# A cosformer attention and MLP-mixer kernel: one load of v moved down its queue, one sum moved behind another, two features moved to ScalarE

## The chip, the cores and the metric

The kernel runs on one core of a Trainium2 chip. The metric is the device time of the kernel in microseconds (us): 267.13 us before the change, the median of 7 runs (266.34 to 269.36). The engines are called PE (TensorE, matrix products), DVE (VectorE), ACT (ScalarE), POOL (GpSimd) and SP (SyncE, which here only issues DMA transfers).

## What is computed

Eight batches (0 to 7 here and in the code, so the seventh is batch 6) of 576 rows and 8 heads of width 64 go through a linear attention, and its output goes through an MLP mixer:

```python
def phi(x, c, s):
    r = np.maximum(x, 0.0)
    return np.concatenate([r * c, r * s], axis=-1)
q_p = phi(q, cos_w, sin_w)
k_p = phi(k, cos_w, sin_w)
kv = np.einsum('bhsf,bhsd->bhfd', k_p, v)
z = np.sum(k_p, axis=2)
num = np.einsum('bhsf,bhfd->bhsd', q_p, kv)
den = np.einsum('bhsf,bhf->bhs', q_p, z)[..., None] + 1e-06
...
h = np.maximum(xt @ w_tok1, 0.0) @ w_tok2
u = x + h.transpose(0, 2, 1)
h2 = np.maximum(u @ w_ch1, 0.0) @ w_ch2
return (u + h2).astype(np.float32)
```

Here x is num/den with the heads side by side (512 channels), and xt is x with rows and channels exchanged. The widths are 256 for the token part (w_tok1, w_tok2) and 1536 for the channel part (w_ch1, w_ch2).

## The kernel before

**Data and tiles.** Each batch has 576 rows: four blocks of 128 rows and a tail of 64. The tails of two batches share a block, so tails are collected in `u_tail` and go through the channel part together at the very end. Inputs are loaded in f32 (k and q into two buffers each, v into one only, `vt`), turned into bf16 features (`kp`, `qp`: relu and a scale by the cosine or sine table, `feat`, lines 445 and 447) and casts (`vbf`, `cast`, line 264).

**Stages of one batch.** `kvm` multiplies features of k with v on PE; `turnx` transposes the q features by DMA into `qpT` (issued by SP, line 469); `numf`/`numfo` give num and den on PE (line 505) and x on DVE (lines 524 to 528); `mix` and `um` are the token part on PE (lines 548 and 575), with B as its hidden layer; `uo` (line 580, DVE) adds x and gives `u`; `ubc` casts `u` to bf16 `ub`, one half on POOL and one on ACT; `utx` transposes each half by DMA into `uT` (line 587, SP). `tm`, `to` and, for odd batches, `tb` do the same for the tail, `tb` with another DMA transpose (line 618). Then comes the channel part of the batch: twelve hidden blocks `c_ps` (line 711), each of four matmuls from `uT` and `wc1`, with a relu by ACT or DVE, and the second layer.

**The second layer as seven products.** The class `Seven` splits the second layer into 2x2 blocks and uses seven products of half size instead of eight (`p1` to `p7`, line 330), with sums on DVE and POOL around them. Each of the products has 12 matmuls of 256 columns. Their order is p1, p4, p2, p5, p6, p7, p3. What matters here: `sums` forms `s1` and `s2` (lines 321, 322), `s3` forms a21 (line 325); p4 ends with the sum into `u21` (line 366, DVE); p2 ends with the sum into `u11` (line 344, DVE); p5 reads `s1`, then ACT copies its result to `vc` (line 370), DVE writes a new `s1` (line 371, the block sum that p3 reads) and POOL adds `vc` to `u22` (line 372). p6 and p7 end with the DVE sums of lines 376, 377, 381 and 384 and a POOL sum (line 383), p3 with line 350. The results p1, p4, p5, p6 and p7 each ask for a bank of PSUM from a pool of four that the hidden blocks use as well.

**What sets the order.** Each engine, and SP's queue of DMA issues, works through its instructions in program order. The program order is written by hand. Up to batch 1's channel part it is the word list `PLAN`: each word is one piece of one batch, and its last letter is the engine (A for ACT, D for DVE, P for POOL). From there on six periods p = 2 to 7 and a tail follow. A period runs `channel` for batch p. It has 20 slots, one after each of the twelve hidden blocks, one after each product and one at the end; `hooks_for` hangs work of other batches on the slots: n = p+1 (numerators, mix, u, `utx` at slots 10 and 12), m = p+2 (casts at slots 3 to 7, features, `turnx` at slots 12, 14 and 15) and the loads of nxt = p+3 (k and q at slot 0, v at slot 16 or 9). The stores of batch p are issued by SP from p7 and p3, slots 17 and 18. The first block `c_ps` of a period needs the whole `uT` of its batch, made in the period before.

The lines around the load of v and around the fourth and fifth product:

```python
at(16 if nxt == 5 else 9, load, nxt, "v")
...
self.product(self.bank("E"), self.a22, t4, True)
nc.vector.tensor_add(self.u21, self.ps["E"], self.u21)
...
self.product(self.bank("C"), self.s1, t1, True)
nc.scalar.copy(self.vc, self.ps["C"])
nc.vector.tensor_sub(self.s1, self.a12, self.s2)
nc.gpsimd.tensor_add(self.u22, self.u22, self.vc)
```

Of the kernel before, what the change touches and what calls it, by code (L numbers as in the profile page):

```python
# [45 lines left out]
up.1.4 upo.1.9.A numf.2.1 up.1.2 numfo.2.1 upo.1.4.A o.0.1 up.1.5 numf.2.0 upo.1.5.A upo.1.2.A numfo.2.0 tq.1.D  # L46
feat.3.q.3.2.0.A feat.3.q.1.2.0.A feat.3.q.2.2.0.A ld.3.v.2.v22 cast.3.4.1.2.P up.1.10 up.1.3 numf.2.2
mix.2.0.2 numfo.2.2 tq.2.D upo.1.10.A up.1.8 up.1.6 numf.2.4 feat.3.q.2.2.1.A upo.1.8.A mix.2.1.2 mix.2.2.2 up.1.1
numfo.2.4 feat.3.q.1.2.1.A mix.2.3.2 mix.2.4.2 mixo.2.2.A feat.3.q.3.2.1.A upo.1.3.D tq.4.D m.1.sums.2.5 turnx.3.2.2
feat.3.q.4.2.1.D upo.1.1.D up.1.7 feat.3.q.0.2.0.A upo.1.6.A up.1.11 upo.1.7.A upo.1.11.A feat.3.k.2.2.0.D  # L50
feat.3.q.4.2.0.A feat.3.q.0.2.1.A turnx.3.4.1 um.2.1 um.2.0 m.1.p1 feat.3.k.4.2.1.A cast.3.1.1.2.P uo.2.1 ubc.2.1 uo.2.0
ubc.2.0 utx.2.1 m.1.sums.0.2 feat.3.k.0.2.1.A m.1.sums.5.6 m.1.s3 turnx.3.0.2 utx.2.0 ld.4.q.2 tb.1
cast.3.0.1.2.A m.1.p4 feat.3.k.0.2.0.A feat.3.k.4.2.0.A cast.3.3.1.2.P m.1.p2 cast.3.2.1.2.P feat.3.k.1.2.0.A
ld.4.v.2.k22 m.1.p5 ld.4.k.2.k32 feat.3.k.2.2.1.A m.1.p6 feat.3.k.3.2.1.A feat.3.k.3.2.0.A feat.3.k.1.2.1.A
m.1.p7 m.1.p3 tm.2 to.2
"""

# [1 line left out]
def kernel(  # L59
# [11 lines left out]
    nc = tc.nc  # L71
# [194 lines left out]
    def relu(eng, dst, src):  # L266
        if eng == "A":
            nc.scalar.activation(dst, src, AF.Relu)  # L268
        else:
            nc.vector.tensor_relu(dst, src)  # L270
# [32 lines left out]
    class Seven:  # L303
# [53 lines left out]
        def p4(self):  # L357
            if self.fine:
                E = [psA.tile([P, D2], F32, name="m2_ps", tag="psA") for _ in range(2)]
                for jj in range(2):  # L360
                    self.product(E, self.a22, t4, True, (jj,))
                    nc.vector.tensor_add(self.u21[:, jj], E[jj], self.u21[:, jj])
                self.store(2, self.u, 2, slice(0, D2))
            else:
                self.product(self.bank("E"), self.a22, t4, True)
                nc.vector.tensor_add(self.u21, self.ps["E"], self.u21)

        def p5(self):
            self.product(self.bank("C"), self.s1, t1, True)
# [327 lines left out]
    def channel(uT, u, store, by_slot, hooks, fine=False):  # L697
        h1 = one.tile([P, NCH, 4 * P], BF16, name="h1")
        m = Seven(h1, u, store, fine)
        slot = 0  # L700

        def step():
            nonlocal slot
            for f in hooks.get(slot, ()):
                f()
            slot += 1

        for mi in range(NCH):
            c_ps = psM.tile([P, 512], F32, name="c_ps", tag="psM")
            for ki in range(NCC):  # L710
                nc.tensor.matmul(c_ps, wc1[:, ki, mi * P:(mi + 1) * P], uT[:, :, ki, :],  # L711
                                 start=(ki == 0), stop=(ki == NCC - 1))
            relu(by_slot[mi], h1[:, mi, :], c_ps)
            if mi == NCH - 2:
                m.sums(0, K2 - 2)
            if mi == NCH - 1:
                m.sums(K2 - 2, K2)
            step()
        order = (m.p1, m.p5, m.p6, m.p7, m.p3, m.p2, m.p4) if fine else (m.p1, m.p4, m.p2, m.p5, m.p6, m.p7, m.p3)
        for f in order:  # L720
            f()
            if f == m.p1:
                m.s3()
            step()
        step()

    bt = [Batch(b) for b in range(B)]
# [10 lines left out]
    def hooks_for(n, m, nxt):  # L738
        h = {}

        def at(slot, f, *a):
            h.setdefault(slot, []).append(lambda: f(*a))
        if nxt is not None:
            at(0, load, nxt, "k")
            at(0, load, nxt, "q")
            at(16 if nxt == 5 else 9, load, nxt, "v")
        if n is not None:
            at(0, n.kv_all)
            for j in range(JA):
                at(2 + j, n.num_all, j)  # L750
            for j in range(JA):
                at(7 + j // 3, n.mix, j, 2)
            at(8, n.mix_out)
            at(10, n.u_all, 0)
            at(10, n.u_all, 1)
            at(12, n.ubc, 1, "A")
            at(12, n.utx, 1)
            at(18, n.u_all, 2)
        if m is not None:
            for j in range(JA):  # L760
                at(3 + j, m.cast, j, 1, 2, "P")
            for i, slot in enumerate((1, 2, 3, 4, 7, 7, 9, 10, 11, 12)):
                at(slot, m.feat, "q", i // 2, 2, i % 2, "A")
            for i, slot in enumerate((7, 7, 8, 8, 13, 14, 15, 16, 17, 17)):
                at(slot, m.feat, "k", i // 2, 2, i % 2, "D" if i < 4 else "A")
            at(12, m.turnx, 0, 2)
            at(14, m.turnx, 2, 2)
            at(15, m.turnx, 4, 1)
        return h
# [3 lines left out]
    for p in range(2, B):  # L773
        s = bt[p]
        n = bt[p + 1] if p + 1 < B else None
        m = bt[p + 2] if p + 2 < B else None
        nxt = p + 3 if p + 3 < B else None
        channel(s.uT, s.u, store_batch(p), evac if n else evac2, hooks_for(n, m, nxt))
    channel(uT_tail, u_tail, store_tail, evac2, {}, fine=True)

    _ = tile, bass_utils
# [30 lines left out]
```

## Time and profile before

| what | us |
|---|---|
| median of 7 runs (lowest, highest) | 267.13 (266.34, 269.36) |
| the profiled execution | 266.49 |
| its span, first to last instruction | 264.7 |
| mean granted clock of PE, as a share | 0.999 |
| period p=2, first block to the next period's | 88.01 to 114.40 |
| period p=3 | 114.40 to 142.02 |
| period p=4 | 142.02 to 168.42 |
| period p=5 | 168.42 to 194.98 |

The profile is of one execution. A row of groups gives an engine, a line of the kernel, an operation with its tiles, how often it ran and for how long. A wait is put down to what came last. The chain of waits goes back from the last instruction, at each step to what released it; the share of PE in it is 84%, of DVE 6% and of DMA 6%. SP is only an issuer: its rows show when a transfer was issued, not when it landed; the time from issue to landing is given apart. Matmuls are pipelined, so the distance between two starts says more than one's length: 0.216 for 512 columns, 0.109 for 256.

### The profile page before, as it was taken

To read this page: it belongs to the slowest core of one execution; us is meant where nothing else is said; L and a number is where in the kernel's file an instruction comes from. 1 tells how busy PE (TensorE), PEld (TensorE's weight loads), DVE (VectorE), ACT (ScalarE), POOL (GpSimd) and SP (SyncE) were. 2 spreads that over 40 slices of the span, in tenths; PEclk is the share of its full clock that TensorE was granted. 3 is DMA by queue.
4 is the path that set the end of the run, shared out by engine and by line. 5 is a ranking of instruction groups with operands and counts; after the bars stand their busy time and mean duration, and the time that the engine had idled before them with its cause. 6 is when DMAs were issued, how large, how long until landed. Compare 5 with 4: busy or idle time off the path is not lost.

```text
span 264.7 us, 5569 instructions
## 1 busy us (share of the span) xinstructions
PE 252.6 (95%) x2201; PEld 164.2 (62%) x2217; DVE 205.4 (78%) x377; ACT 150.7 (57%) x244; POOL 62.1 (23%) x78
## 2 busy tenths in 40 slices
PE   6887999999999999999998999999999999999993
PEld 2776556456558655865585548754875486486482
DVE  6389797799999787879885868886878488476484
ACT  2787263473779396948683778586854342323320
POOL 2083070040036112321436002440230023003020
PEclk9999999999999999999999999999999999999999
DMA  6999999999979999999999997950594042202104
GB/s 199 360 249 172 256 263 234 365 217 256 370 209 172 250 350 387 229 191 324 291 318 202 283 368 176 162 195 2 106 173 160 2 79 96 85 0 85 76 1 160
DMA packets 79434, 53.41 MB, mean 202 GB/s; under 512 B 47792, under 2 KB 77232, under 8 KB 79408
## 3 DMA queue, kind: packets, MB, share of 16 engines
q1 hardware_dynamic: 74688, 48.77, 69.2%
q0 software_dynamic: 4144, 3.77, 9.4%
q10 hardware_dynamic: 576, 0.52, 0.6%
q8 instruction: 17, 0.28, 0.4%
q14 instruction: 9, 0.07, 0.1%
HBM read 35.85 MB, written 9.44 MB: 171 GB/s over the span
## 4 chain that ended last, share of the span: by engine, by line
PE 84%; DVE 6%; DMA 6%; issue 2%; DVEq 0%
PE c_ps L711 28%; PE m_ps L330 22%; PE c L627 8%; PE b L548 6%; PE u L575 5%; PE kv L476 4%; PE o L639 4%; DMA kt<-in_k_dram 3%; PE nf L505 3%; DMA uT<-ub 3%; DVE kp L447 1%; PE tr L460 1%; PE ut L603 1%; PE nm L505 1%; DVE x L528 1%
## 5 line engine op out<-in xcount | busy, mean ns | idle before, releaser
L711 PE MATMUL c_ps<-uT,wc 128*128 128x512 bf16 x288 | 70.4, 379 | 1.1 <-DMA uT<-ub 1.1
L268 ACT ACTIVATE h<-c_ps 128x512 bf16<-128x512 f32 x66 | 38.8, 595 | 50.8 <-PE c_ps L711 36.2
L711 PEld LDWEIGHTS <-wc 128*128 128x128 bf16 x336 | 30.6, 97 | 34.0 <-issue 2.0
L330 PEld LDWEIGHTS <-h 128*128 128x128 bf16 x384 | 37.5, 98 | 6.1
L445 ACT ACTIVATE qp<-qt,cos_t 128x512 bf16<-128x512 f32 x35 | 24.7, 720 | 15.0 <-DMA qt<-in_q_dram 11.8
L330 PEld LDWEIGHTS <-s 128*128 128x128 bf16 x288 | 28.0, 98 | 4.1 <-DVE s L371 0.7
L264 POOL CAST vbf<-vt 128x512 bf16<-128x512 f32 (+3 forms) x29 | 19.2, 699 | 45.1 <-DMA vt<-in_v_dram 45.1
L270 DVE TENSOR_SCALAR h<-c_ps 128x512 bf16<-128x512 f32 x18 | 12.4, 688 | 19.7 <-PE c_ps L711 19.7
L264 POOL CAST ub<-u 128x1024 bf16<-128x1024 f32 x9 | 9.7, 1075 | 68.5 <-DVE u L580 68.4
L330 PE MATMUL m_ps<-wc,s 128*128 128x256 bf16 x192 | 23.6, 273 | 0.4 <-DVE s L371 0.4
L330 PE MATMUL m_ps<-wc,h 128*128 128x256 bf16 x192 | 23.6, 273 | 0.0
L330 PE MATMUL m_ps<-t,h 128*128 128x256 bf16 x192 | 23.6, 273 | 0.0
L445 ACT ACTIVATE qp<-qt,sin_t 128x512 bf16<-128x512 f32 x32 | 22.9, 721 | 0.0
L627 PE MATMUL c<-uT,wc 128*128 128x512 bf16 x96 | 22.7, 379 | 0.1
L528 DVE TENSOR_TENSOR x<-nf,den 128x512 bf16<-128x512 f32 x30 | 20.7, 691 | 1.0
L505 PEld LDWEIGHTS <-qpT 128*128 128x128 bf16 x320 | 15.3, 98 | 9.6 <-DVE x L528 1.5
L548 PE MATMUL b<-x,w 128*128 128x512 bf16 (+1 forms) x84 | 19.8, 354 | 0.3
L580 DVE TENSOR_TENSOR u<-u,x 128x1024 f32<-128x1024 f32 x16 | 18.9, 1217 | 0.9 <-PE u L575 0.8
L372 POOL TENSOR_TENSOR u<-u,vc 128x512 f32<-128x512 f32 x7 | 9.5, 1356 | 35.4 <-ACT vc L370 35.4
L445 ACT ACTIVATE kp<-kt,sin_t 128x512 bf16<-128x512 f32 x23 | 16.0, 713 | 1.7 <-DVE u L580 1.5
L447 DVE TENSOR_SCALAR kp<-kt,cos_t 128x512 bf16<-128x512 f32 x18 | 10.6, 596 | 8.1 <-DMA kt<-in_k_dram 8.1
L445 ACT ACTIVATE kp<-kt,cos_t 128x512 bf16<-128x512 f32 x22 | 15.3, 712 | 0.8 <-DMA kt<-in_k_dram 0.8
(117 smaller groups left out, 389.9 us busy)
## 6 DMA issues: line engine op xcount, KB each, us to landing
out_dram<-u SPq DMA_DIRECT2D x32, 256.0 KB, 3.3
qt<-in_q_dram SPq DMA_DIRECT2D x8, 640.0 KB, 7.6
kt<-in_k_dram SPq DMA_DIRECT2D x8, 640.0 KB, 8.2
qt<-in_q_dram SPq DMA_DIRECT2D x8, 512.0 KB, 6.5
kt<-in_k_dram SPq DMA_DIRECT2D x8, 512.0 KB, 7.1
vt<-in_v_dram SPq DMA_DIRECT2D x6, 640.0 KB, 8.8
vt<-in_v_dram SPq DMA_DIRECT2D x6, 512.0 KB, 7.4
wc<-in_moe_w_ch_dram POOLq DMA_DIRECT2D x4, 384.0 KB, 8.1
```

The costliest lines, as they stand in the source:

```text
L264: (nc.scalar.copy if eng == "A" else ENG[eng].tensor_copy)(dst, src)
L268: nc.scalar.activation(dst, src, AF.Relu)
L330: nc.tensor.matmul(ps[jj] if isinstance(ps, list) else ps[:, jj], a[:, ki, jj * P:(jj + 1) * P], b[:, ki], start=(first and ki == 0 and (j ...
L445: nc.scalar.activation(dst, src, AF.Relu, scale=tab)
L447: ENG[eng].tensor_scalar(dst, src, scalar1=tab, scalar2=0.0, op0=ALU.mult, op1=ALU.max)
L505: nc.tensor.matmul(nm[:, hh * (D + 1):(hh + 1) * (D + 1)], self.qpT[:, j * H + h, :], self.kv[:, h, :D + 1], start=(not eps or hh == 0), s ...
L528: nc.vector.tensor_mul(dst, nmv[:, :, :, :D], den_b)
L548: nc.tensor.matmul(b1[:, mi], w1[:, col(self.c, j), mi * P:(mi + 1) * P], self.x[:, j, cs], start=(j == 0 and (g == 2 or mi == 0)), stop=( ...
L575: nc.tensor.matmul(ps[:, jj], w2[:, ki, 1 + 2 * g + jj, :], self.B1[:, ki, :], start=(ki == 0), stop=(ki == NT - 1))
L580: nc.vector.tensor_add(self.sb("u")[:, js, :], self.ps.pop(("u", g)), self.x[:, js, :])
L627: nc.tensor.matmul(ps, wc1[:, ki, mi * P:(mi + 1) * P], self.uT[:, :, ki, :], start=(ki == 0), stop=(ki == NCC - 1))
L711: nc.tensor.matmul(c_ps, wc1[:, ki, mi * P:(mi + 1) * P], uT[:, :, ki, :], start=(ki == 0), stop=(ki == NCC - 1))
```

## The change

Three edits. The load of v for batch 6 (nxt = 6, issued in period p=3) goes from slot 9 to slot 16; batch 5's stays at 16 and batch 7's at 9. The sum into `u21`, which ended p4, becomes a function of its own, `u21_out`, and is called after p5, without a slot of its own, in every period and in the plan; the tail (`fine`) keeps its own. In the plan two features of batch 3 go from DVE to ACT and stand earlier: `feat.3.q.4.2.1` and `feat.3.k.2.2.0`, now ahead of the last two pieces of batch 2's mix.

```diff
-numfo.2.4 feat.3.q.1.2.1.A mix.2.3.2 mix.2.4.2 mixo.2.2.A feat.3.q.3.2.1.A upo.1.3.D tq.4.D m.1.sums.2.5 turnx.3.2.2
-feat.3.q.4.2.1.D upo.1.1.D up.1.7 feat.3.q.0.2.0.A upo.1.6.A up.1.11 upo.1.7.A upo.1.11.A feat.3.k.2.2.0.D
+numfo.2.4 feat.3.q.1.2.1.A feat.3.k.2.2.0.A feat.3.q.4.2.1.A mix.2.3.2 mix.2.4.2 mixo.2.2.A feat.3.q.3.2.1.A upo.1.3.D tq.4.D m.1.sums.2.5 turnx.3.2.2
+upo.1.1.D up.1.7 feat.3.q.0.2.0.A upo.1.6.A up.1.11 upo.1.7.A upo.1.11.A
...
-ld.4.v.2.k22 m.1.p5 ld.4.k.2.k32 feat.3.k.2.2.1.A m.1.p6 feat.3.k.3.2.1.A feat.3.k.3.2.0.A feat.3.k.1.2.1.A
+ld.4.v.2.k22 m.1.p5 m.1.u21_out ld.4.k.2.k32 feat.3.k.2.2.1.A m.1.p6 feat.3.k.3.2.1.A feat.3.k.3.2.0.A feat.3.k.1.2.1.A
...
                 self.product(self.bank("E"), self.a22, t4, True)
-                nc.vector.tensor_add(self.u21, self.ps["E"], self.u21)
+
+        def u21_out(self):
+            nc.vector.tensor_add(self.u21, self.ps["E"], self.u21)
...
-        order = (m.p1, m.p5, m.p6, m.p7, m.p3, m.p2, m.p4) if fine else (m.p1, m.p4, m.p2, m.p5, m.p6, m.p7, m.p3)
+        order = (m.p1, m.p5, m.p6, m.p7, m.p3, m.p2, m.p4) if fine else (m.p1, m.p4, m.p2, m.p5, m.u21_out, m.p6, m.p7, m.p3)
         for f in order:
             f()
             if f == m.p1:
                 m.s3()
-            step()
+            if f != m.u21_out:
+                step()
...
-            at(16 if nxt == 5 else 9, load, nxt, "v")
+            at(9 if nxt == 7 else 16, load, nxt, "v")
```

## The prediction

> **What bounds the kernel now.** I read the page's busy table first, then PE's waits, then the chain of waits around each of them, then SP's issue timeline.
>
> ```profile
> PE 252.6 (95%) x2201; PEld 164.2 (62%) x2217; DVE 205.4 (78%) x377; ACT 150.7 (57%) x244; POOL 62.1 (23%) x78
> ```
>
> PE is busy for 252.6 of 264.7 us and holds 84% of the chain: another engine counts only where it makes PE wait. PE's waits from 60 us to the end are two:
>
> ```profile
> PE c_ps L711 <- DMA uT<-ub: 1.1, 1, 1.1
> PE m_ps L330 <- DVE s L371: 0.4, 1, 0.4
> ```
>
> Matmul ends are modelled, so I measure the loss between starts. At the first, the single `ut` matmul started at 140.58 and `c_ps` at 142.02; undisturbed (168.21 to 168.42) that step is 0.21. Loss 1.23 us. At the second, the last matmul of `p7` started at 85.41 and `p3` at 86.09, where 0.11 is normal. Loss 0.57 us. These two are all that this change can take away. The chain around the first (start, us, what):
>
> ```profile
> 131.35 3.71 PE m_ps L330 x35
> 135.07 6.82 DMA uT<-ub
> 141.89 0.14 issue
> 142.02 1.02 PE c_ps L711 x4
> ```
>
> The period p=4 starts when the second half of batch 4's `uT` lands at 141.89, 6.82 us after its issue. The same transpose one period later, issued at 162.06, took 3.3. SP's issues show why:
>
> ```profile
> 116.86 1.29 SPq L143 DMA_DIRECT2D vt<-in_v_dram  x2
> 118.27 2.88 SPq L282 DMA_DIRECT2D out_dram<-u  x4
> 121.25 1.94 SPq L618 DMA_TRANSPOSE uT_tail<-utb  x1
> 123.28 1.43 SPq L143 DMA_DIRECT2D kt<-in_k_dram  x2
> 124.77 2.54 SPq L143 DMA_DIRECT2D qt<-in_q_dram  x2
> 128.27 1.89 SPq L143 DMA_DIRECT2D vt<-in_v_dram  x2
> 133.09 5.20 SPq L587 DMA_TRANSPOSE uT<-ub  x2
> ```
>
> Batch 5's v (116.86), the stores, batch 6's k and q and then batch 6's v (128.27) stand ahead of the two `utx` in one queue. The second half of that v was issued at 128.91 and landed 9.5 later, at 138.4; the transposes landed behind it, at 139.4 and 141.9. From 128 to 134 the engines moved 355 GB/s at a share above 1: full.
>
> **Part 1, batch 6's v from slot 9 to slot 16 of p=3.** It removes from before `utx` two DMAs of 640 and 512 KB, 1.18 MB, 3.3 us at 355 GB/s. The last load ahead is then q of batch 6, issued at 126.01 and landed 9.2 later, at 135.2. In p=2, where no v stands there, the last q landed at 110.8 (101.09 + 9.7) and the second `uT` at 112.5: 1.75 behind it. Behind the v it was 3.45. So `uT` lands between 136.9 and 138.7, and PE can use it at 140.79: over 2 us early. The stall goes whole: -1.23.
>
> What is late next? At slot 16 the v goes behind the three `turnx` (slots 12, 14, 15) and ahead of the stores of batch 3, batch 7's k and q (slot 0 of p=4) and batch 7's v (slot 9), each 1.29 to 2.5 us of issue as above. Three things wait behind it. POOL's casts of batch 6 ran at 141.2; PE needs them at the start of p=5, near 168. The stores of batch 3 must leave `u` before L580 of p=4, near 157. In p=3 the same order landed them by 127.4, 13 us into the period: 154. Batch 7's v waits until the casts have emptied the one `vt` buffer. That is the order that p=3 has now, one period later. I shift its rows by 26.4 (from 114.40 to p=4's new start, 140.79): casts end near 154.6, v lands at 138.4 + 26.4 = 164.8. Off this comes the tail's transpose at 121.25, which p=3 doesn't have between its stores and p=4's k: in six slices of 0.275 us around 126.4 DMA moved 121 GB/s on the mean instead of 355, a loss of 1.1 us. So v lands near 163.7 at the latest, and up to 1 us earlier, since the `turnx` are no longer held up (in p=5 their issue ended 27.7 into the period, in p=2 28.8). `uT` of batch 5 follows by 2.4 to 3.45: 165.1 to 167.2. PE needs it by 167.06 (168.42 - 1.23, less 0.13 from landing to matmul). Ends: a wait of 0.1, or 1.9 to spare. I take none, because most of this interval is early.
>
> POOL's five casts then run near 150 to 154, against DVE's k features, as they did at 124.6 to 128.2 in p=3 (0.80 instead of 0.61 each), and no PE wait was seen there: 0.
>
> **Part 2, `u21` sum behind the block sum.** From p=2 on, L371 (`s1`) waits for PE, not DVE: at 110.24 DVE had idled 0.32 before it. So `s1` isn't earlier. The sum (0.68, L366) moves from before L344 to after L371 and pushes L376 from 111.55 to about 111.8, as DVE idled 0.35 there. The next sums follow 0.2 later; L350 ended at 116.06 and PE had no wait behind it. I put 0 on this, below nothing too: no wait of PE there ends on DVE. If the cover went, 0.2 a period, 1.2 in six.
>
> In the written-out plan DVE is late:
>
> ```profile
> 83.29 0.68 DVE u L366
> 83.97 0.60 DVE u L344
> 84.56 1.48 DVE s L371
> 86.05 0.05 issue
> 86.09 1.48 PE m_ps L330 x12
> 87.58 0.05 issue
> 87.63 0.39 PE ut L603
> 88.02 1.01 PE c_ps L711 x4
> ```
>
> L371 could start 0.60 earlier, at 83.89. The rows of its two engines:
>
> ```profile
> 84.49 1.55 DVE L371 TENSOR_TENSOR s<-h,s 128x1536 bf16<-128x1536 bf16 x1
> 83.95 1.27 POOL L372 TENSOR_TENSOR u<-u,vc 128x512 f32<-128x512 f32 x1 [1.39 <-ACT vc L370]
> ```
>
> L371 took 1.55 beside POOL and 0.96 in the later periods: it finished 0.82 after POOL let go at 85.22. [...] That speaks against the move: the new start is only 0.06 ahead of POOL's. If DVE comes first, `s1` is ready at 84.85 and PE loses nothing at 85.52 (-0.57); if POOL does, it's ready at 86.04 as now (0).
>
> I take 0 either way, for another wait ends last. PE would reach `c_ps` 0.57 earlier than 87.85, at 87.27. But that block needs the last `uT` of batch 2, issued at 84.43 and landed 3.4 later, at 87.87; already now `c_ps` starts 0.17 late on it (88.01, where 87.63 + 0.21 would be free). Its SP queue runs back to back from 78.74 (`turnx`, `utx`, `turnx`, `utx`), released by a q feature on ACT (L445, `feat.3.q.4.2.0`, 77.98 to 78.72) that the change doesn't move. So the DVE wait turns into a DMA wait with the same end. Bounds: -0.57 to 0.
>
> **Part 3, two features to ACT.** DVE loses two L447 of 0.48 (at 75.39 and 76.39). Next is L580 at 76.99, which waits for PE's first four `u` matmuls, started at 75.93 and ended by 76.96; so the DVE chain behind it keeps its times: 0. ACT gets two of 0.72, 0.62 apart, 1.24 together, placed ahead of the relu to B at 74.40, before which ACT idled 2.14 waiting for PE. The k data landed at 71.5 (63.18 + 8.3), before 72.2 where they'd start. 0.9 of cover stays; were it gone, B, `u` and all behind would move by what is missing. 0.
>
> **Sum.** -1.23 + 0 + 0. The profiled execution took 266.49 (span 264.7 and 1.8 around it), 0.64 below the median of 267.13. 266.49 - 1.23 = 265.26; as a median 265.9.
>
> **The rivals.**
> The stall moves to p=5's start. For it: the late-v-then-early-v order that made it is now in p=4, and my margin there has an end at 0.1 late; a dip in transpose traffic like that near 140.4 (under 10 GB/s) would add up to 1. Against it: no tail transpose, earlier `turnx`. Gives back 0.6 to 1.2: 266.5 to 267.1. Chance 0.23.
>
> Or the plan's wait goes too. That needs batch 2's last `uT` to land 0.6 earlier; against it, its queue is back to back. 265.3. Chance 0.10.
>
> The slower one is a bank. `p7` takes the PSUM bank freed first; with four banks and `p4`'s sum read late, it could take that one and wait for the moved sum. In each of six periods the sum would end near 111.8 where `p7` started at 111.35: 0.5, so 3.0; in the plan 85.44 against 84.21, 1.2. +4.2 - 1.23: 270.1. It decides at whether `p7` gets `p4`'s bank or `p1`'s, freed by the earlier sum L344. Against it: at the tail's start the second block began at 241.61 and was not held by L350, which ran to 242.89, so banks go by when they were freed, not in turn; with the sum moved, `p1`'s comes free first. Chance 0.07.
>
> The likeliest, 265.9, has 0.60; its own range is 265.4 to 266.4 by the runs' scatter.
>
> **How the numbers follow.** Half a per cent, about what a measurement of this kernel can tell from no change, is 1.34 us: faster means below 265.8. Half of the likeliest case lies below (0.30), with the plan's wait 0.40. Same: the other 0.30 and the moved stall, 0.53. Slower: the bank, 0.07. The range runs from 265.0 (plan's wait gone, some scatter) to 267.3 (whole stall moved).
>
> **What would show it.** Right: no PE wait on `uT` at p=4's start, `uT` of batch 4 landed by 138.7, `c_ps` of p=4 at about 140.8; batch 6's v issued near 143 behind `turnx`; batch 5's `uT` landed before 167. In the plan `s` L371 at 83.9, no PE wait on it, and p=2's first `c_ps` still at 88.0, now waiting 0.6 for `uT`. Wrong: a PE wait on `uT` near 167, `c_ps` of p=2 before 87.9, or `p7` waiting for L366.

## The result and the profile after

The changed kernel takes 265.94 us (median of 25 runs, 264.99 to 267.2); the kernel before, run beside it, 267.34 (60 runs). The ratio is 0.995, interval 0.9936 to 0.9964: 1.4 us faster by the medians, between 1.0 and 1.7 by the interval. The forecast was 265.9. The profiled execution took 265.70 with a span of 263.9, 0.79 less than the one before.

A number that fits doesn't make its steps right, so the profile is read in the same order. PE's waits from 60 us on (engine and line, what it waited for: us, times, longest):

```profile
PE c_ps L713 <- ACT h L268: 0.5, 1, 0.5
PE m_ps L330 <- DVE s L373: 0.3, 1, 0.3
```

The wait on `uT` is gone. The wait on the block sum is still there (0.3 where it was 0.4), and a wait on an ACT relu is new. (Lines behind 366 stand two or three lower in the changed file: L371 is now L373, L711 is L713.) SP's issues of the two periods:

```profile
132.83 2.63 SPq L589 DMA_TRANSPOSE uT<-ub  x2
135.55 7.95 SPq L471 DMA_TRANSPOSE qpT<-qp  x3
143.55 1.29 SPq L143 DMA_DIRECT2D vt<-in_v_dram  x2
...
154.37 1.87 SPq L143 DMA_DIRECT2D vt<-in_v_dram  x2
159.23 4.74 SPq L589 DMA_TRANSPOSE uT<-ub  x2
164.06 7.64 SPq L471 DMA_TRANSPOSE qpT<-qp  x3
```

In p=3 the `utx` now stand right behind q of batch 6, the second lands at 139.30, 1.24 before `c_ps` of p=4 needs it, and the period takes 26.39 instead of 27.62. In p=4 batch 7's v is issued at 154.37, when the late batch 6's v has been cast, and the transposes of both kinds come behind it. The chain around p=5's new wait:

```profile
169.24 0.69 PE c_ps L713 x4
169.93 3.71 DMA qpT<-qp
...
173.82 0.72 ACT qp L447
174.54 0.49 ACT h L268
175.04 0.04 issue
175.08 1.02 PE c_ps L713 x4
```

Read it from below: PE's block waited for a bank that ACT's relu (174.54) had to free; that relu stood behind a q feature of batch 7 (173.82), which may only write `qp` when the last `turnx` of batch 6 has read it, and that landed at 173.64. It costs 0.67: p=5 takes 27.06 where it takes 26.39 undisturbed. ACT's row of that feature, in the profile of before and in the changed one:

```profile
173.20 0.72 ACT L445 ACTIVATE qp<-qt,cos_t 128x512 bf16<-128x512 f32 x1 [0.98 <-DMA qpT<-qp]
173.82 0.72 ACT L447 ACTIVATE qp<-qt,cos_t 128x512 bf16<-128x512 f32 x1 [3.09 <-DMA qpT<-qp]
```

In the plan the chain is almost the one of before:

```profile
83.23 0.68 DVE u L344
83.91 1.74 DVE s L373
85.66 0.05 issue
85.70 1.48 PE m_ps L330 x12
87.19 0.05 issue
87.24 0.38 PE ut L605
87.62 0.13 issue
87.74 1.02 PE c_ps L713 x4
```

The `u21` sum is out of the chain and L373 starts right behind L344, but it takes 1.81 instead of 1.55:

```profile
83.83 1.81 DVE L373 TENSOR_TENSOR s<-h,s 128x1536 bf16<-128x1536 bf16 x1
83.56 1.27 POOL L374 TENSOR_TENSOR u<-u,vc 128x512 f32<-128x512 f32 x1 [1.05 <-ACT vc L372]
```

POOL's sum had started ahead of it, at 83.56, and ended at 84.83; L373 ended 0.81 after that. p=2's first block starts at 87.74, 0.14 after the last `uT` of batch 2 landed at 87.61.

### The profile page after: what moved, and what is told of

It is laid out like the page before. It is cut to its first block, busy times and chain, and to the rows that moved or that the text cites. A ratio compares the mean times of both kernels' runs of the same rounds, so it can differ in the third digit from the quotient of the medians.

```text
span 263.9 us, 5567 instructions
## 1 busy us (share of the span) xinstructions
PE 253.5 (96%) x2201; PEld 164.6 (62%) x2217; DVE 206.3 (78%) x375; ACT 151.8 (58%) x246; POOL 62.4 (24%) x78
## 4 chain that ended last, share of the span: by engine, by line
PE 85%; DVE 7%; DMA 4%; issue 2%; ACT 0%; ACTq 0%; DVEq 0%
PE c_ps L713 26%; PE m_ps L330 25%; PE c L629 8%; PE b L550 6%; PE u L577 5%; PE kv L478 4%; PE o L641 4%; DMA kt<-in_k_dram 3%; PE nf L507 3%; DMA qpT<-qp 1%; PE ut L605 1%; PE tr L462 1%; DVE kp L449 1%; PE nm L507 1%; DVE u L582 1%
## 5 line engine op out<-in xcount | busy, mean ns | idle before, releaser
L713 PE MATMUL c_ps<-uT,wc 128*128 128x512 bf16 x288 | 70.4, 379 | 0.6 <-ACT h L268 0.5
L713 PEld LDWEIGHTS <-wc 128*128 128x128 bf16 x336 | 30.8, 97 | 33.4 <-issue 1.2
L330 PEld LDWEIGHTS <-s 128*128 128x128 bf16 x288 | 27.9, 98 | 3.9 <-DVE s L373 0.5
L447 ACT ACTIVATE qp<-qt,sin_t 128x512 bf16<-128x512 f32 x33 | 23.6, 720 | 0.0
L447 ACT ACTIVATE kp<-kt,cos_t 128x512 bf16<-128x512 f32 x23 | 16.0, 712 | 0.5 <-DMA kt<-in_k_dram 0.5
```

The costliest lines, as they stand in the source:

```text
L330: nc.tensor.matmul(ps[jj] if isinstance(ps, list) else ps[:, jj], a[:, ki, jj * P:(jj + 1) * P], b[:, ki], start=(first and ki == 0 and (j ...
L447: nc.scalar.activation(dst, src, AF.Relu, scale=tab)
```

## The experiments

All ratios are to the kernel before, run beside each experiment on the same chip; the experiments ran on several chips, so ratios compare better than times. The theory after this profile: A, the load makes the whole difference, and sum and features bring nothing. The rival: B, they bring part.

**The change once more.**

> The changed kernel once more, to see how far its profile repeats. If the waits are the kernel's own: no PE wait on uT at p=4's start, and again 0.6 to 0.7 us of PE waiting for ACT's relu near 174 us in p=5. If the 0.39 us by which PE ran ahead from 16 us on was scatter of the first loads, it differs in this run. Time 0.4 to 0.7% below before.

265.81 us, 0.9949 (0.9925 to 0.9973). In its profile p=3 takes 26.39 again, and p=5 has the ACT wait again, but 0.36. PE's lead of 0.39 from 16 us on is not there: the plan's first down-projection product starts at 43.89, against 43.72 before and 43.33 in the first profile of the change. Over all the profiles here it starts between 43.09 and 43.89: that is scatter between executions.

**The load alone.** The edit, against the kernel before:

```diff
-            at(16 if nxt == 5 else 9, load, nxt, "v")
+            at(9 if nxt == 7 else 16, load, nxt, "v")
```

> Only batch 6's v goes from slot 9 to slot 16; sum and features stay as before. Theory A, the load makes the whole difference: 1.23 us of PE's wait on uT go, about 0.67 come back as a wait on ACT in p=5, the same time as with all three edits within 0.3 us. Theory B, the sum and the features bring part: slower than all three edits by 0.4 us or more.

266.45, 0.9954 (0.993 to 0.9977), and the second time:

> Only batch 6's v at slot 16, once more: the first time it was 0.46% below before, all three edits 0.51%. If sum and features bring nothing, 0.4 to 0.6% below again; if they bring 0.5 us, 0.3%. In its profile the transposes of batch 6 land some 5.8 us into p=5 and PE doesn't wait for ACT there, as in the first, or 6.4 to 6.7 and it does, as in the change: that tells whether that wait belongs to the edits or to the run.

265.96, 0.9964 (0.994 to 0.9989). p=3 takes 26.39 in both profiles. So the load alone brings the gain, as A says; a few tenths more by the other edits can't be excluded, since the intervals overlap. But A missed one thing that it had named: in neither profile does PE wait in p=5. The last `turnx` of batch 6 landed 5.84 and 5.90 into p=5, where in the change it landed at 6.70 and 6.40. So that wait is not of the load alone.

**Sum and features without the load.** The edit, against the changed kernel:

```diff
-            at(9 if nxt == 7 else 16, load, nxt, "v")
+            at(16 if nxt == 5 else 9, load, nxt, "v")
```

> Only the sum behind the block sum and the two features on ACT; batch 6's v stays at slot 9. Theory A: no difference from before, within 0.3 us; the wait on uT at p=4's start stays at 1.1 us or more, and p=2's first block starts with the last uT of batch 2. Theory B: faster than before by 0.4 to 0.8 us.

269.48, 1.0089 (1.0057 to 1.0122): both theories missed. These two edits cost 2 us where the load still stands in front. The trace says where:

```profile
PE c_ps L713 <- DMA uT<-ub: 2.1, 1, 2.1
```

The last `uT` of batch 4 lands 28.5 after p=3's start, not 27.5, so p=3 takes 28.64. And p=4, with no wait in it, takes 27.92 instead of 26.40.

**Which of the two, and why two periods.** From here theory D: the features do it, by moving a fetch of program into the transposes; rival E: the sum does it.

> Only the sum behind the block sum; load of v and features as before. The two edits together were 0.9% slower, with the last uT of batch 4 landing at 143.2 instead of 141.9 and PE's clock at 0.7 in the slice after it. Theory D: only the instruction stream of ACT or DVE decides, by when its next piece of program is fetched (the 8 KB packets of queue 14), and it's the features, not the sum, that add ACT instructions: no difference from before within 0.3 us. Theory E: the sum itself brings the loss, 1.5 to 2.5 us slower.

267.28, 0.999 (0.9961 to 1.002). No difference. (In its profile p=3 took 27.99, p=4 26.40. PE also waited 0.72 for `uT` of batch 2 at p=2's start, where no other trace has over 0.48; what made that is open.)

> Only the two features on ACT, as in the change; load of v and sum as before. Theory D: 1.5 to 2.5 us slower than before, a fetch of queue 14 near 141 us while uT of batch 4 is transposed, where before it had one at 145.3. Theory E: no difference within 0.3 us.

269.67, 1.0075 (1.0038 to 1.0112). The features bring the loss, alone. The windows 141 to 144 and 144 to 147 of this run (after the stretch: us; busy time of PE, PE's weight loads, DVE, ACT and POOL; granted clock of PE, DMA share, GB/s):

```profile
141.00:144.00 3.00, 1.14 (x3) 0.43 (x4) 1.84 (x3) 0.00 (x0) 3.00 (x6) 0.82 1.28 241
144.00:147.00 3.00, 3.00 (x45) 2.44 (x44) 0.00 (x0) 0.85 (x2) 0.34 (x1) 0.61 1.14 224
```

PE idled 2.3 us, and then its granted clock was 0.5 for 3.4 us, from 142.9 to 146.4: p=3 takes 28.67, p=4 27.95. In the trace of before, where PE idled 1.2 us, the clock stays at 1.00 in both windows. Then the DMA engines from 141 to 143 us, in slices of 0.05 us:

```profile
GB/s 92 256 302 287 297 282 292 287 287 396 256 292 256 282 261 282 282 302 271 102 10 10 10 10 10 10 10 10 113 256 276 307 271 302 287 292 287 297 297 276
...
q14 instruction: 1, 0.01, 1.0%
```

A packet of queue 14, of kind "instruction", came at 141.5, and from 142.0 to 142.4 the transposes stood still at 10 GB/s, while the second half of `uT` was being moved. In all three runs with the features and the early load this packet came between 141.2 and 141.9 and `uT` landed 28.5 to 28.7 into p=3; in the two without the features it came at 145.3 and 146.9, behind `uT`, which landed at 27.5 and 27.9. Counted from the landing of batch 6's v, `uT` came 3.8 to 4.0 later in the three and 3.4 to 3.5 in the two.

**The clock apart from the landing.** Sum and features, early load, and nine matmuls on a zero tile in the time in which PE waits (added work, result unused; the diff shows the matmuls alone):

```diff
+        if p == 4:
+            keep_warm(9)
         channel(s.uT, s.u, store_batch(p), evac if n else evac2, hooks_for(n, m, nxt))
```

> Sum and features with the v load at slot 9, as in the run that was 0.9% slower, and nine matmuls on a zero tile (1.94 us, result unused) ahead of p=4's first block, in the time in which PE waited for uT. If the idle stretch of 2 us costs clock behind it (kv's 40 matmuls ran 0.07 us further apart there, 1.3 us in all), this is 1.0 to 1.5 us faster than without the nine, with the same landing of uT. Rival: the landing alone is late and the clock was scatter: same time as without them.

268.34, 1.0019 (0.9987 to 1.005), where the run without the nine had 1.0089 (1.0057 to 1.0122). In its profile p=3 takes 28.78, so `uT` is just as late, and p=4 26.40:

```profile
141.00:144.00 3.00, 2.72 (x27) 1.32 (x25) 1.66 (x3) 0.26 (x1) 3.00 (x5) 1.00 1.22 225
144.00:147.00 3.00, 3.00 (x48) 1.93 (x45) 0.06 (x1) 1.53 (x3) 0.16 (x1) 1.00 1.12 216
```

The halved clock was worth 1.5 us in p=4, and the idle stretch before it was its cause. The timed executions say the same. Of the 12 with the features alone, 7 have a mean granted clock of 0.989 to 0.992 and a median of 269.89, the other 5 have 0.997 to 0.998 and 268.39: 1.5 us apart. Of the 12 with the nine matmuls none is below 0.996. So about 1 us of the loss is the late landing (268.39 against 267.47 of the kernel before beside it), and 1.5 us comes on top where the clock falls. The slow stretch with the features alone lasted 3.41 us. An idle stretch of 2.3 us came ahead of the halved clock in two traces (the features alone; sum and features); behind one of 1.6 us (the sum alone) p=4 took its 26.40.

**The fetch apart from the features.** The features on ACT alone, and ten tiny copies on ACT while it waits for the first loads (added work, result unused; the diff shows the copies alone):

```diff
     nc.scalar.activation(cos_t, theta, AF.Sin, bias=bias_hp, scale=-scale)
+    pad = const.tile([P, 1], F32, name="pad")
+    for _ in range(10):
+        nc.scalar.copy(pad, bias0)
```

> Only the two features on ACT, as in the run that was 0.75% slower, and ten tiny copies (one element a partition, result unused) on ACT while it waits for the first loads. If the fetch of queue 14 near 141 us is ACT's program and its place is what made the transposes late, ten more instructions pull it some 6 us or more ahead, out of the transposes of uT; uT of batch 4 lands 0.4 to 0.5 earlier in the period (about 28.1 instead of 28.5 after p=3's start), PE idles under 2 us, the clock stays at 1.0, and the time is within 0.5 us of before. Rival: the fetch stays, or goes and nothing changes: 1.5 to 2.5 us slower than before again.

267.03, 0.998 (0.9953 to 1.0007): the loss of 2 us is gone with ten more instructions on ACT. The packet of queue 14 now came at 136.7, ahead of the transposes of `uT`; `uT` landed 27.1 into p=3, p=3 took 27.21, the clock stayed at 1.0:

```profile
PE c_ps L714 <- DMA uT<-ub: 0.7, 1, 0.7
```

So the work of the features, which is still there, is not what costs; what ten early instructions on ACT move decides. Part of that is the packet: `uT` now lands 3.3 behind batch 6's v. But of the gain in landing, 1.4 us, the standstill explains 0.4; batch 6's v landed 0.9 earlier as well, and what moved that is open. That the packet brings ACT's program is argued from its moving with ACT's instructions; the record names no engine for it.

**The new wait in p=5.** First by its source, batch 7's v (both diffs are against the changed kernel):

```diff
-            at(9 if nxt == 7 else 16, load, nxt, "v")
+            at(16, load, nxt, "v")
```

> All three edits, and batch 7's v at slot 16 of p=4 too. Theory A says that the new wait of p=5 comes from batch 7's v, which stands ahead of batch 6's transposes: with it behind them turnx of batch 6 lands within 5 us of p=5's start, the wait of 0.67 goes, and the kernel is 0.5 to 0.7 us faster than with the three edits. Rival C, the wait is moved on: the casts of batch 7 come late and PE waits for them at p=6's start, or nothing is gained.

265.52, 0.9926 (0.9902 to 0.9951). `turnx` of batch 6 land 4.61 into p=5, p=5 takes 26.39, and no later period is longer. Then by its place, ACT's queue:

```diff
-                at(slot, m.feat, "q", i // 2, 2, i % 2, "A")
+                at(slot + 3 if m.b == 7 and slot < 5 else slot, m.feat, "q", i // 2, 2, i % 2, "A")
```

> The change, and in p=5 the first four q features of batch 7 three slots later (4 to 7 instead of 1 to 4). If the new wait in p=5 is ACT standing in its queue at the first of them until turnx of batch 6 has read qp, it's gone, 0.3 to 0.7 us faster than the change. Rival: PE waits elsewhere for the same transposes (qpT in nf), no gain.

265.46, 0.9914 (0.9883 to 0.9946). The transposes land as late as in the change (6.76), but p=5 takes 26.60: the relus at 172.29 and 173.41 no longer stand behind the feature. The 0.20 left is PE's own wait for `qpT`.

```profile
172.29 0.60 ACT L268 ACTIVATE h<-c_ps 128x512 bf16<-128x512 f32 x1 [0.72 <-PE c_ps L713]
173.41 0.60 ACT L268 ACTIVATE h<-c_ps 128x512 bf16<-128x512 f32 x1 [0.52 <-PE c_ps L713]
173.90 0.71 ACT L447 ACTIVATE qp<-qt,cos_t 128x512 bf16<-128x512 f32 x1
```

**All loads late, without sum and features.** The edit, against the kernel before:

```diff
-            at(16 if nxt == 5 else 9, load, nxt, "v")
+            at(16, load, nxt, "v")
```

> All loads of v at slot 16, sum and features as before. If sum and features bring nothing once the transposes are free of the loads, this equals all three edits with all loads at 16 (0.7 to 0.8% below before) within 0.3 us. Rival: sum and features are worth 0.4 us or more there, and this is slower by that.

265.3, 0.9932 (0.9902 to 0.9961): the same as with them, by both interval and periods (26.39 to 26.40 throughout). This one edit, and the two runs above, have no PE wait left behind p=2 but that 0.20; by time they lie 0.3 us or more below the change, but the intervals overlap, so that they are faster than it isn't shown.

**The block sum and POOL.** The change without batch 1's POOL sum, so that its result is not the kernel's:

```diff
+            self.pool_sum = True
...
-            nc.gpsimd.tensor_add(self.u22, self.u22, self.vc)
+            if self.pool_sum:
+                nc.gpsimd.tensor_add(self.u22, self.u22, self.vc)
...
+                self.seven.pool_sum = False
```

> The change, but batch 1's sum of vc into u22 on POOL (line 374 there) is left out, for batch 1 alone: work left out, so that nothing on POOL runs beside the block sum in the plan. If POOL is what holds the block sum (1.81 us in the changed kernel, 0.96 undisturbed), it takes 0.96 and PE's wait for it before p3 goes. Theory A: the next wait is uT of batch 2 (first block of p=2 starts 0.13 after its landing, as before), so the time is that of the change within 0.3 us. Rival: 0.4 us faster.

265.31, 0.9927 (0.9899 to 0.9954); the change lies within that interval, so time alone decides nothing. The trace does:

```profile
84.54 0.94 DVE L374 TENSOR_TENSOR s<-h,s 128x1536 bf16<-128x1536 bf16 x1
```

0.94 instead of 1.81, PE's wait before `p3` is gone, and p=2's first block still starts 0.14 after `uT` of batch 2 (87.84), 44.38 after the first down-projection product, where the change has 44.42. (PE waited 0.41 before `p7` instead.) This run also lacks the wait in p=5; its `turnx` landed at 6.01. Nor does it need work left out: in the run with the nine matmuls DVE's block sum came first by itself (83.44, POOL's at 83.50) and took 0.94, and p=2's first block still started 0.13 after `uT` of batch 2.

## Why the prediction was right, and where it was not

**The load, -1.23: right, in place and size.** p=3 went from 27.62 to 26.39 in every run with the load at slot 16. `uT` of batch 4 landed at 139.30, 0.6 behind the 136.9 to 138.7 of the text, with 1.2 to spare: from 137.6 to 139.2 the transposes stood still, as they had from 140.3 in the profile of before. Batch 6's v was issued at 143.55, as said.

**What is late next in p=4: the step that failed.** I followed batch 7's v to the casts, the stores and `uT` of batch 5, and those came as worked out: v landed at 164.16 (163.7 at the latest was said), `uT` at 165.96 with 0.98 to spare. I did not follow the third user of the queue, `turnx` of batch 6, to the first q feature of batch 7 on ACT. In the profile of before that feature already waited 0.98 for the same transfer (the first of the two ACT rows above), so the place to look was there; 1.4 us of cover were left. The landing from p=5's start and PE's loss, run by run: 4.60 and 0 (before), 5.84 and 0, 5.90 and 0 (load alone), 6.01 and 0 (without the POOL sum), 6.40 and 0.36, 6.70 and 0.67 (the change). The loss is what goes beyond about 6.03. The term was 0 in the sum and measured 0.36 and 0.67.

**The sum, 0: right.** Alone it makes 0.999 (0.9961 to 1.002). In the change p=6 and p=7 take 26.40 and 19.53, as before; the bank rival is excluded: `p7` has no wait in any of the six periods.

**In the plan, 0: right, and for the reason given.** The text left open who comes first, DVE or POOL; in the change it was POOL, so `s1` was ready no earlier, and the sign named for it (no PE wait on the block sum) did not come. Where DVE came first, or POOL's sum was left out, `s1` was ready in time, and the first block of p=2 still stood behind `uT`.

**The features, 0: right in this change, wrong as a statement about the edit.** The engines' time was hidden, as said: ACT idled there and DVE's next step waited for PE. What was not in the sum is that with two instructions moved between engines a packet of kind "instruction" came at another time (141.5 us in the run with the features alone, 145.3 before). With the early load the move costs 2 us (1.0075), through a later landing (28.5 to 28.7 into p=3 instead of 27.5 to 27.9) and the clock that fell to 0.5 behind it. With the late load `uT` is through before, and what can still be seen is that the two load-only runs had `turnx` at 5.84 and 5.90, while the change had 6.40 and 6.70 (6.76 with the q features later). A fetch inside that last `turnx` does not make the difference: without the POOL sum one came there (171.0) and they landed at 6.01; with the q features later it came before that `turnx` was issued (168.6), and they landed at 6.76. The lateness is older: in the three late runs batch 6's v landed 10.05 to 10.45 into p=4 and batch 7's v was issued at 13.83 to 14.22, in the other three at 9.33 to 9.96 and 12.91 to 13.74. What delays batch 6's v there, and whether it is the features, is open.

**The sum of it.** -1.23 and +0.36 to +0.67 make -0.56 to -0.87 by the traces; the runs say -1.0 to -1.7. Before has one trace, and its p=3 (27.62) need not be the usual one: the sum-only run, with the same load order and the same time, had 27.99. The fallen clock is not what is missing: of the 94 executions of the kernel before that ran beside the experiments, 7 have a granted clock of 0.993 or less (the two traces with a halved stretch have 0.990 and 0.992), and without them the median is still 267.26. A wait that is mostly longer than in the one trace could be it, but the timed executions left no trace, so this stays open. That 265.9 was hit to 0.1 is therefore partly luck: the wait that I missed was made up for by a gain larger than the one I summed from the trace.

## What to carry to other kernels

A load that is moved down a queue shifts every user behind its new place: list them all, transposes of the next batch included, and look up for each how much of its wait is still covered. What an edit costs can depend on another edit: the features lost 2 us with the load in front and nothing that shows behind it, so parts are to be measured together and apart. And an idle stretch of PE can cost more than its length (here one of 1.6 us cost nothing further, and one of 2.3 us another 1.5 us at half the clock): count the slow clock that may follow it, not the stretch alone.

## What the runs showed of the hardware

Transposes by DMA stood still (under 40 GB/s) behind most packets of kind "instruction" that fell among them. In the profile of before this began 0.4 to 0.9 us after the start of five 16 KB packets of queue 8 and lasted 1.1 to 1.4 us (1.1 from 140.3, behind the packet at 139.59); over all the traces it was 0.5 to 1.8 us (1.6 from 137.5 in the changed kernel), and 0.35 to 0.8 us behind the 8 KB packets of queue 14 (0.35 from 140.75 and 0.8 from 170.55 in the changed kernel, 0.4 from 142.0 with the features alone). It was not so behind every one: the packet of queue 14 at 145.30 in the profile of before, among transposes too, was followed by 0.2 us only; and gaps also came with no packet near (1.1 us from 162.9 in the changed kernel). Plain loads ran on across such a packet (at 153.8 in the profile of before, with a mean of 369 GB/s from 153.5 to 155.5).

An idle stretch of PE of 2.3 us, in the run with the features alone, was followed by half its granted clock for 3.41 us; p=4 took 27.95 instead of 26.40, 1.5 us more. Behind the 1.2 us of before the clock stayed at 1.00.

DVE's block sum took 0.94 to 0.96 where no instruction of POOL ran at its start (0.96 in the later periods of before, 0.94 without the POOL sum). In ten traces it started in the plan while a sum or cast of POOL ran; it then took 1.25 to 2.00 and ended 0.81 to 0.82 after POOL's instruction in every one (before: 1.55 and 0.82; the change: 1.81 and 0.81). Where it started first, in the run with the nine matmuls, it took 0.94 and POOL's sum 2.01 instead of 1.27. My reading of these figures: the later of the two waited for the earlier one to end, rather than both running slower.
